# Wider rows for V, an earlier turn of one K tile, and two weight loads in another place

## The chip, the cores and the metric

The kernel runs on one core of one Trainium2 chip. The metric is device microseconds of one execution. All runs quoted here are of the fast state, with a granted TensorE clock of 0.997 to 1.0. A profile's span is 1.8 to 1.9 us shorter than the time of the same execution (188.6 us and 190.53 us for the profile of before). Engine names in the profile: PE is TensorE (matmul), PEld its weight loads, DVE VectorE, ACT ScalarE, POOL GpSimd, SP the engine that issues most loads.

## The reference

It is grouped-query attention over the last 2048 positions of a cache, with the projections before and after it.

```python
B, Sq, D = 8, 32, 1024;  Hq, Hkv, Sk, Dh = 32, 4, 8192, 128;  W = 2048
q = (x @ wq)                      # 8 query heads share one K/V head
scores = einsum(q, k_cache[:, :, Sk - W:]) * Dh ** -0.5
p = softmax(scores)
o = einsum(p, v_cache[:, :, Sk - W:])
out = o @ wo
```

There are 32 pairs of batch and K/V head, called units here. A unit has 256 query rows, 2048 keys and 512 KB each of K and V in bf16.

## The kernel before

The kernel takes a unit in four chunks ("slots") of 512 keys. In each slot TensorE computes four score matmuls, ScalarE takes the exponential, and two slots later TensorE multiplies by V in eight matmuls. V gets a column of ones, so the same matmuls also give the sum of the softmax: a row of V has 129 elements, 258 bytes.

```python
self.VW = self.Dh + 1                                    # 129
self.va = [self.c1.tile([P, self.KT, self.VW], BF16, name=f"va{i}") for i in range(3)]
...
for jj in range(CJ):                                     # the four rows of V of a chunk
    j = c * CJ + jj
    for qt in range(QT_N):                               # two matmuls with the same row of V
        nc.tensor.matmul(o_ps[:, qt, 0:self.VW], lhsT=pT[:, jj, qt * P:(qt + 1) * P], rhs=va[:, j, :], ...)
```

The score matmuls read K transposed. For most units the DMA transposes it. For units 0 to 4 TensorE does, and for units 5, 8, 11, ... the tile is turned beside TensorE: VectorE transposes blocks in four pieces (`kb`), then 16 moves put the blocks in place (`kTv`). For unit 5 GpSimd does twelve of the moves and VectorE four. A table names the slots:

```python
# unit: (load of K with that of unit .., blocks from, moves from, moves until, moves by GpSimd)
V_T = {5: (2, 6, 12, 17, 12), ...}
spread(blocks, s0, s1 + (s1 - s0) // 3)                  # unit 5: slots 6, 8, 10, 12
spread(moves, s1, s2)                                    # unit 5: slots 12 to 16
```

Projections for the next group of heads and output projections are cut into pieces and put between the slots. Their weights come by the same load queue as K and V; the n-th 512 KB of weights is issued after the loads of unit `W_AT[n]`:

```python
W_AT = (2, 3, 4, 4, 8, 8, 9, 10, 11, 12, ...)            # first four: group 1; next four: group 2
```

## Time and profile before

| | before |
|---|---|
| time, median of 3 runs | 189.4 us |
| span of the profiled execution | 188.6 us |
| PE busy | 181.3 us (96%) |
| ACT, DVE, POOL busy | 70%, 61%, 50% |
| idle gaps of PE, ended by DMA, POOL, DMA | 0.34, 0.71, 0.69 us |

From the page of before, its first two parts; a digit is the busy share of one fortieth of the span, in tenths:

```profile
PE 181.3 (96%) x2048; PEld 154.5 (82%) x2064; DVE 115.2 (61%) x267; ACT 131.9 (70%) x133; POOL 94.2 (50%) x150
PE   7999999989999899999999999999999999999993
```

PE is never far from full. Apart from the first and the last slice, its line has two weak ones, at 38 us and at 63 us. From the view of waits of before (who waited for whom; total us, times, longest us), the lines of PE, without that of the warm-up at the start (1.2 us):

```profile
PE s_ps L462 <- POOL kTv L255: 0.7, 1, 0.7
PE q_ps L269 <- DMA wq_sb<-in_wq_dram: 0.7, 1, 0.7
PE tp L230 <- DMA k_raw<-in_k_cache_dram: 0.3, 1, 0.3
```

Three stretches of the timeline of before show each of them (start, length, engine, line, operation, tiles; in brackets the idle time before it and what ended it):

```profile
24.66 0.34 PE L230 MATMUL tp<-ident,k_raw 128*128 128x128 bf16 x3 [0.34 <-DMA k_raw<-in_k_cache_dram]
...
30.54 8.37 POOL L255 TENSOR_SCALAR kTv<-kb 32x512 bf16<-32x512 bf16 x12 [28.97 <-PE o_ps L473]
...
38.96 0.28 PE L462 MATMUL s_ps<-QT_63,kTv 128*128 128x256 bf16 x1 [0.71 <-POOL kTv L255]
...
63.75 0.39 PE L269 MATMUL q_ps<-xT,wq_sb 128*128 128x256 bf16 x2 [0.69 <-DMA wq_sb<-in_wq_dram]
```

A gap in this view is shorter than what it costs, because a matmul's end is modelled and lies past the start of the next one (a matmul on V is 220 ns long in the profile, and the next one starts 56 to 61 ns after it). From start to start, less the usual distance, the three cost 0.50, 0.87 and 0.85 us.

The matmuls on V look alike in every view (median 220 ns each), but with the next start 56 to 61 ns on, that length is not what one costs. So the distance between starts says more. From the trace's records of before, mean ns from the start of a V matmul to the start of the next (the last one of a chunk is followed by other work, so that the figure of the second in row 3 comes from the one place where two chunks follow each other):

```text
row of the chunk           0      1      2      3
first matmul of the row   56.7   60.8   60.1   59.6
second                    56.6   55.9   55.9   56.0
```

### The profile page before, as it was taken

To read this page: it belongs to the slowest core of one execution; us is meant where nothing else is said; L and a number is where in the kernel's file an instruction comes from. 1 tells how busy PE (TensorE), PEld (TensorE's weight loads), DVE (VectorE), ACT (ScalarE), POOL (GpSimd) and SP (SyncE) were. 2 spreads that over 40 slices of the span, in tenths; PEclk is the share of its full clock that TensorE was granted. 3 is DMA by queue.
4 is the path that set the end of the run, shared out by engine and by line. 5 is a ranking of instruction groups with operands and counts; after the bars stand their busy time and mean duration, and the time that the engine had idled before them with its cause. 6 is when DMAs were issued, how large, how long until landed. Compare 5 with 4: busy or idle time off the path is not lost. (4 is left out here: it accounts for less than half of the span.)

```text
span 188.6 us, 5054 instructions
## 1 busy us (share of the span) xinstructions
PE 181.3 (96%) x2048; PEld 154.5 (82%) x2064; DVE 115.2 (61%) x267; ACT 131.9 (70%) x133; POOL 94.2 (50%) x150
## 2 busy tenths in 40 slices
PE   7999999989999899999999999999999999999993
PEld 2889989979999799987878899987787888888842
DVE  0137889994595485487367648756755865355272
ACT  2218889767789687878787686787777888888700
POOL 2000004959929939947963990697199279600000
DMA  4999999999999999999899999989999899960012
GB/s 161 301 384 412 402 402 386 201 233 335 301 198 280 378 264 293 358 262 290 284 377 207 363 380 292 275 289 386 257 368 333 231 260 287 272 149 0 3 59 63
DMA packets 52507, 51.75 MB, mean 274 GB/s; under 512 B 39424, under 2 KB 40064, under 8 KB 52480
## 3 DMA queue, kind: packets, MB, share of 16 engines
q1 hardware_dynamic: 51904, 50.87, 96.3%
q10 hardware_dynamic: 576, 0.52, 0.8%
q8 instruction: 17, 0.28, 0.6%
q14 instruction: 10, 0.08, 0.1%
HBM read 41.42 MB, written 0.52 MB: 222 GB/s over the span
## 5 line engine op out<-in xcount | busy, mean ns | idle before, releaser
L464 ACT ACTIVATE pT<-s_ps 128x1024 bf16<-128x1024 f32 x128 | 129.0, 1025 | 36.5 <-PE s_ps L462 35.5
L255 POOL TENSOR_SCALAR kTv<-kb 32x512 bf16<-32x512 bf16 x140 | 93.3, 666 | 68.7 <-PE o_ps L473 29.0
L473 PEld LDWEIGHTS <-pT 128*128 128x128 bf16 x1024 | 69.3, 98 | 3.1
L462 PEld LDWEIGHTS <-kT 128*128 128x128 bf16 x368 | 34.8, 98 | 10.3
L289 PE MATMUL op_ps<-wo_sb,OT 128*128 128x512 bf16 (+1 forms) x120 | 32.9, 365 | 0.8
L269 PE MATMUL q_ps<-xT,wq_sb 128*128 128x256 bf16 x192 | 28.3, 273 | 0.7 <-DMA wq_sb<-in_wq_dram 0.7
L473 PE MATMUL o_ps<-va_112,pT 128*128 128x129 bf16 x352 | 27.5, 220 | 0.0
L473 PE MATMUL o_ps<-va_113,pT 128*128 128x129 bf16 x352 | 27.3, 220 | 0.1
L473 PE MATMUL o_ps<-va_114,pT 128*128 128x129 bf16 x320 | 25.0, 220 | 0.0
L245 DVE STREAM_TRANSPOSE kb<-k_raw 128x512 bf16<-128x512 bf16 x36 | 23.9, 685 | 0.0
L411 DVE RECIPROCAL RL_all<-o_ps 128x2 f32<-128x2 f32 x32 | 5.3, 166 | 29.5 <-PE o_ps L473 29.2
L416 DVE TENSOR_SCALAR o_sb<-o_ps,RL_all 128x128 bf16<-128x128 f32 x64 | 19.5, 347 | 1.1
L462 PEld LDWEIGHTS <-kTv 128*128 128x128 bf16 x144 | 13.8, 98 | 6.1 <-POOL kTv L255 1.0
L269 PEld LDWEIGHTS <-wq_sb 128*128 128x128 bf16 x192 | 16.9, 98 | 2.1 <-DMA wq_sb<-in_wq_dram 1.0
L462 PE MATMUL s_ps<-QT_63,kT 128*128 128x256 bf16 x112 | 16.8, 273 | 0.0
L418 DVE STREAM_TRANSPOSE OT<-o_sb 128x256 bf16<-128x256 bf16 x32 | 14.3, 445 | 1.1
L462 PE MATMUL s_ps<-QT_66,kT 128*128 128x256 bf16 x96 | 14.4, 273 | 0.1
L289 PEld LDWEIGHTS <-OT 128*128 128x128 bf16 x136 | 11.1, 97 | 2.8 <-DVEq L76 0.6
L462 PE MATMUL s_ps<-QT_65,kT 128*128 128x256 bf16 x80 | 12.0, 273 | 0.1
L462 PE MATMUL s_ps<-QT_64,kT 128*128 128x256 bf16 x80 | 12.0, 272 | 0.1
L296 DVE TENSOR_TENSOR oacc<-op_ps,oacc 128x512 f32<-128x512 f32 x8 | 5.5, 682 | 7.5 <-PE op_ps L289 7.5
L405 DVE COPY va_113<-v_sb 128x2048 bf16<-128x2048 bf16 x11 | 9.0, 820 | 0.0
(46 smaller groups left out, 105.6 us busy)
## 6 DMA issues: line engine op xcount, KB each, us to landing
v_sb<-in_v_cache_dram SPq DMA_DIRECT2D x32, 512.0 KB, 7.3
wo_sb<-in_wo_dram SPq DMA_DIRECT2D x16, 512.0 KB, 6.7
wq_sb<-in_wq_dram SPq DMA_DIRECT2D x14, 512.0 KB, 7.5
k_raw<-in_k_cache_dram SPq DMA_DIRECT2D x13, 512.0 KB, 7.2
wq_sb<-in_wq_dram SPq DMA_DIRECT2D x4, 256.0 KB, 6.6
kT<-in_k_cache_dram SPq DMA_TRANSPOSE x36, 7.1
k_raw<-in_k_cache_dram SPq DMA_DIRECT2D x2, 256.0 KB, 7.9
x_sb<-in_x_dram ACTq DMA_DIRECT2D x1, 256.0 KB, 3.8
```

The costliest lines, as they stand in the source:

```text
L245: nc.vector.transpose(out=st["kb"][:, sl, :], in_=self.k_raw[ui][:, sl, :])
L255: nc.gpsimd.tensor_scalar(out=out, in0=in_, scalar1=1.0, scalar2=1.0, op0=ALU.mult, op1=ALU.mult)
L269: nc.tensor.matmul(st["ps"][:, 0:self.NQ], lhsT=self.wq_t[g, i][:, c % (DC // 2), hl * P:(hl + 1) * P], rhs=self.xT[:, c, :], start=(c == ...
L289: nc.tensor.matmul(ps[:, 0:w], lhsT=self.OT[:, gq, c, t * P:(t + 1) * P], rhs=self.wo_t[gq][:, c, n0:n0 + w], start=(k == 0), stop=(k == 7))
L296: nc.vector.tensor_tensor(out=acc, in0=ps[:, 0:w], in1=acc, op=ALU.add)
L405: self.nc.vector.tensor_copy(out=self.va[ui % 3][:, :, 0:self.Dh], in_=self.v_sb[ui][:, :, :])
L411: nc.vector.reciprocal(out=rl[:, ui * QT_N:(ui + 1) * QT_N], in_=o_ps[:, :, Dh])
L416: nc.vector.tensor_scalar(out=o_sb[:, qt, :, :], in0=o_ps[:, qt, 0:Dh].rearrange("p (i c) -> p c i", c=4), scalar1=rl[:, ui * QT_N + qt:ui ...
L418: nc.vector.transpose(out=self.OT[:, g * QT_N:(g + 1) * QT_N, :, b * self.Sq:(b + 1) * self.Sq], in_=o_sb[:, :, :, :])
L462: nc.tensor.matmul(s_ps[:, jj, :], lhsT=self.kT[ui][:, c * CJ + jj, :], rhs=q_u, start=True, stop=True)
L464: nc.scalar.activation(out=pT[:, :, :], in_=s_ps[:, :, :], func=ACT.Exp, bias=0.0, scale=self.scale)
L473: nc.tensor.matmul(o_ps[:, qt, 0:self.VW], lhsT=pT[:, jj, qt * P:(qt + 1) * P], rhs=va[:, j, :], start=(j == 0 and qt == 0), stop=(j == KT ...
```

## The change

It has four parts: a row of V becomes 160 elements (320 bytes), so that every row starts on a multiple of 64 bytes of its tile; the four block transposes of unit 5 move from slots 6, 8, 10, 12 to 5, 6, 8, 10, and its moves begin in slot 10 instead of 12; the first weights of group 1 are loaded behind K and V of unit 3 instead of unit 2; the last weights of group 2 behind the loads of unit 9 instead of 10.

```diff
+VA_ROW = 160
-V_T = {5: (2, 6, 12, 17, 12), ...
+V_T = {5: (2, (5, 6, 8, 10), 10, 17, 12), ...          # the other units keep their slots
-W_AT = (2, 3, 4, 4, 8, 8, 9, 10, 11, ...
+W_AT = (3, 3, 4, 4, 8, 8, 9, 9, 11, ...
-        self.va = [self.c1.tile([P, self.KT, self.VW], BF16, name=f"va{i}") for i in range(3)]
+        self.va = [self.c1.tile([P, self.KT, VA_ROW], BF16, name=f"va{i}") for i in range(3)]
...
-            spread(blocks, s0, s1 + (s1 - s0) // 3)
+            for k, p in enumerate(blocks):
+                plan[s0[k]].append(p)
...
-    ... rhs=va[:, j, :],
+    ... rhs=va[:, j, 0:self.VW],
```

More of the change, by code (lines that the diff above doesn't have):

```diff
@@ L20 @@
 N_WARM = (7, 0, 0)
+VA_ROW = 160
 PE_T = (0, 1, 2, 3, 4)
-V_T = {5: (2, 6, 12, 17, 12),
-       **{u: (u - 4, 4 * u - 16, 4 * u - 13, 4 * u - 4, 16) for u in (8, 11, 14, 17, 20, 23, 26, 29)}}
-W_AT = (2, 3, 4, 4, 8, 8, 9, 10, 11, 12, 13, 13, 14, 15, 16, 16, 18, 19, 19, 20, 22, 22, 23, 24, 25, 26, 28, 28)
+V_T = {5: (2, (5, 6, 8, 10), 10, 17, 12),
+       **{u: (u - 4, range(4 * u - 16, 4 * u - 12), 4 * u - 13, 4 * u - 4, 16) for u in (8, 11, 14, 17, 20, 23, 26, 29)}}
+W_AT = (3, 3, 4, 4, 8, 8, 9, 9, 11, 12, 13, 13, 14, 15, 16, 16, 18, 19, 19, 20, 22, 22, 23, 24, 25, 26, 28, 28)
 Q_SLOTS = {1: (17, 31), 2: (38, 54), 3: (69, 83)}
@@ L472, in pv @@
                         for qt in range(QT_N):
-                            nc.tensor.matmul(o_ps[:, qt, 0:self.VW], lhsT=pT[:, jj, qt * P:(qt + 1) * P], rhs=va[:, j, :],
+                            nc.tensor.matmul(o_ps[:, qt, 0:self.VW], lhsT=pT[:, jj, qt * P:(qt + 1) * P], rhs=va[:, j, 0:self.VW],
                                              start=(j == 0 and qt == 0), stop=(j == KT - 1), skip_group_check=True)
```

## The prediction

> **What bounds the kernel.** TensorE. The page has PE busy 181.3 of 188.6 us (96%), and the view of waits has three idle gaps of PE after the start-up: 0.34 us for the DMA of K of unit 3 (tp from k_raw, at 24.66 us), 0.71 us for GpSimd's last move of K of unit 5 (kTv, at 38.96), 0.69 us for the last weights of group 2 (wq_sb, at 63.75). Matmul ends overlap; by start-to-start intervals from the records those three cost 0.50, 0.87 and 0.85 us, 2.2 us together.
>
> **What the change does.**
>
> 1. *Weights of group 1 behind K and V of unit 3.* Early 512 KB loads land every 1.3 us (weights at 23.34, K of unit 3 at 24.62). K of unit 3 now lands near 23.4; PE needs it near 24.1. The 0.50 us goes. K of unit 4, next, still lands at 28.51, wanted near 28.55: no spare.
>
> 2. *Turn of unit 5 sooner.* GpSimd's 12 moves run from 30.54 to 38.91 (0.70 us each), behind VectorE's fourth transpose at 29.67. With that one in slot 10 it ends near 28.1, the moves near 36.5, and unit 5 is wanted near 37.5. The 0.87 us goes.
>
> 3. *Weights of group 2 one load sooner.* Issued at 57.77, they landed at 63.70; issued near 51, they land near 58.5. The 0.85 us goes. K of unit 14 lands 1.3 us later.
>
> 4. *Rows of 320 bytes.* The matmul on 129 columns of V runs 1024 times. From start to start it takes 56.6 ns for rows 0, 4, 8, 12 of V, whose byte offset (258 times the row) is a multiple of 8, but the first of each pair on the other rows takes 60.9, 60.1 and 59.5 ns (the second about 56). Per chunk of four rows that is 8.6 ns, in 128 chunks 1.1 us, all on PE. I take it for misalignment, which rows of 320 bytes remove. [...] The rival: the pattern follows the place within the chunk, also of period four; then nothing is gained. VectorE's copies of V (655 to 1090 ns) stay off the critical path.
>
> **What may be given back.** DMA engines are near 100% busy from 5 to 165 us (slices); loads hardly move with PE. The smallest spare time of V before its copy is 1.8 us (unit 16, landing 93.07, copy 94.87). PE will be about 2.8 us ahead there, so VectorE will wait about 1 us for V of units 15 to 17 and for K of units 14 and 20; PE itself has over 2 us more, so I count only 0.1 to 0.2 us.
>
> **Sum.** 189.4 - 2.2 - 1.0 + 0.2 = 186.4 us. Eight in ten: 185.7 to 187.6; near 187.3 if point 4 fails. Chances: faster by over 2% 0.12, within 2% 0.87, slower 0.01.
>
> **What would show it.** PE has no gap over 0.1 us near 24, 38 and 63; unit 5's first scores start near 37.4 instead of 38.96; groups of eight V matmuls start evenly at about 56.5 ns; the median of the copies of V stays near 690 ns.
>
> **What would make it wrong.** The row pattern is not alignment; VectorE, fully busy from 34 to 40 us, delays the earlier turn; K of unit 4 or V of unit 16 becomes the new wait, so that stalls move instead of going.

## The result, and the profile after

The changed kernel took 187.25 us (median of 6 runs, 187.13 to 187.44) against 189.41 us for the kernel before in the same rounds (6 runs, 188.68 to 189.69). The ratio is 0.989, with a 95% interval of 0.9871 to 0.9908. Here and below a ratio is the mean time of one kernel's fast runs over that of the other's fast runs of the same rounds, so it is not quite the ratio of the medians. The gain is 2.2 us. I had predicted 3.0 us: the time lies in the stated range (185.7 to 187.6), 0.85 us above its centre.

The page of after, the same two lines:

```profile
PE 178.8 (96%) x2048; PEld 153.1 (82%) x2064; DVE 115.1 (62%) x267; ACT 131.7 (71%) x133; POOL 94.7 (51%) x150
PE   7699999999999999999999999999999999999993
```

The weak slices at 38 and 63 us are gone; one in the start (4.6 to 9.3 us) is new. All lines of PE in the view of waits of after:

```profile
PE q_ps L372 <- DMA wq_sb<-in_wq_dram: 1.4, 1, 1.4
PE warm_ps L342 <- DVE wz L311: 1.2, 1, 1.2
```

The three waits of before are no longer there. The 1.4 us are in the first projection, at 6.8 us, where nothing was changed. The timeline of after at the places of the two large waits (start, length, as above):

```profile
28.59 8.78 POOL L256 TENSOR_SCALAR kTv<-kb 32x512 bf16<-32x512 bf16 x12 [27.02 <-DMA k_raw<-in_k_cache_dram]
...
37.65 0.60 PE L464 MATMUL s_ps<-QT_63,kTv 128*128 128x256 bf16 x4
...
61.25 0.60 PE L270 MATMUL q_ps<-xT,wq_sb 128*128 128x256 bf16 x4
```

GpSimd's moves begin 1.95 us sooner and end at 37.37 us; PE takes up unit 5 at 37.65 without a wait. It is a close fit: 0.29 us to spare, where I had expected 1.0. VectorE's fourth block transpose, for which the moves wait, before and after:

```profile
29.67 0.70 DVE L245 STREAM_TRANSPOSE kb<-k_raw 128x512 bf16<-128x512 bf16 x1
```

```profile
27.74 0.69 DVE L246 STREAM_TRANSPOSE kb<-k_raw 128x512 bf16<-128x512 bf16 x1
```

And the starts of the V matmuls, from the records of after:

```text
row of the chunk           0      1      2      3
first matmul of the row   56.6   56.5   56.7   56.6
second                    56.7   56.8   56.7   56.0
```

So in the profiles all four parts did what they were meant to do, and the spans differ by 3.0 us (188.6 and 185.6), exactly the gain I had predicted. That match is chance: after began its first score matmul 0.23 us later than before (13.65 and 13.43 us), and from there on the two differ by 3.27 us. The timed runs differ by 2.2 us only. That is the question for the experiments: 0.8 us that is in the pair of profiles and not in the pair of times. The profile of before belongs to an execution of 190.53 us, 1.1 us above the median of its timed runs.

Theory 1: the profile of before shows an unusual execution, in which loads were late; its two waits for a DMA (0.50 and 0.85 us) are not there in most runs. Theory 2: the waits are always there, and a part of the gain is lost elsewhere.

### The profile page after: what moved, and what is told of

Read it like the earlier page. It is cut to its first block, busy times and chain, and to the rows that moved or that the text cites. A ratio compares the mean times of both kernels' runs of the same rounds, so it can differ in the third digit from the quotient of the medians.

```text
span 185.6 us, 5054 instructions
## 1 busy us (share of the span) xinstructions
PE 178.8 (96%) x2048; PEld 153.1 (82%) x2064; DVE 115.1 (62%) x267; ACT 131.7 (71%) x133; POOL 94.7 (51%) x150
## 5 line engine op out<-in xcount | busy, mean ns | idle before, releaser
L475 PEld LDWEIGHTS <-pT 128*128 128x128 bf16 x1024 | 68.5, 98 | 3.1
L475 PE MATMUL o_ps<-va_112,pT 128*128 128x129 bf16 x352 | 27.1, 220 | 0.0
L475 PE MATMUL o_ps<-va_113,pT 128*128 128x129 bf16 x352 | 27.0, 220 | 0.1
L475 PE MATMUL o_ps<-va_114,pT 128*128 128x129 bf16 x320 | 24.7, 220 | 0.0
L406 DVE COPY va_113<-v_sb 128x2048 bf16<-128x2048 bf16 x11 | 9.5, 859 | 0.0
```

The costliest lines, as they stand in the source:

```text
L406: self.nc.vector.tensor_copy(out=self.va[ui % 3][:, :, 0:self.Dh], in_=self.v_sb[ui][:, :, :])
```

## The experiments

All twelve runs gave correct results. Each is the kernel before with the one edit shown, unless said otherwise. They ran in four jobs on four chips (4, 10, 12 and 14), each compared with before on the same chip. A gain in us is worked out from the ratio, unless said otherwise. "Cost" of a wait below is always from start to start.

### Which of the waits are there in every run

**before_again: the kernel before, profiled once more.** No edit.

> The kernel before, unchanged, profiled once more. Question: the change was worth 2.2 us in timed runs, 3.0 us between the two profiles, and I had predicted 3.0. Theory 1 (the profile of before that I costed from was of a slow run, 190.5 us against a median of 189.4, with loads landing every 1.29 us instead of 1.25): a profile of a usual run shows the same start intervals of V matmuls (56.6 and about 60 ns), the POOL gap of about 0.7 us near 38 again, but the two gaps that a DMA ends (0.34 near 24.7 and 0.69 near 63.7) smaller, all three together 1.0 to 1.4 us instead of 2.2. Theory 2 (the stalls are the same in every run, and part of the gain is lost elsewhere): the three gaps are again 2.2 us by start intervals. Time: 1.00 of before under both.

Measured: 189.66 us against 189.40, ratio 1.0011 (0.9995 to 1.0027). The view of waits of this second profile, the lines of PE but those of the start:

```profile
PE s_ps L462 <- POOL kTv L255: 0.7, 1, 0.7
```

The timeline of the second profile at the three places, K of unit 3, the turn of unit 5 and the weights of group 2:

```profile
24.44 0.39 PE L230 MATMUL tp<-ident,k_raw 128*128 128x128 bf16 x4
...
38.73 0.61 PE L462 MATMUL s_ps<-QT,kTv 128*128 128x256 bf16 x4 [0.71 <-POOL kTv L255]
...
62.45 0.60 PE L269 MATMUL q_ps<-xT,wq_sb 128*128 128x256 bf16 x4
```

The wait for GpSimd is there again, with the same cost (0.88 us). Both waits for a DMA are gone without any change of the kernel. The last weights of group 2 landed at 61.32 us instead of 63.70, before PE wanted them. The three together cost 0.88 us instead of 2.2, even less than theory 1 had said. From the first scores to the end of the span the two profiles of the same kernel took 175.21 us (188.64 - 13.43) and 173.84 us (187.54 - 13.70): a difference of 1.37 us, where the two missing waits are 1.35. The later jobs recorded the span of 44 executions of the kernel before, 186.8 to 188.1 us: the profile I had costed from, at 188.6, lies outside all of them.

**turn5_only: the earlier turn alone.**

```diff
-V_T = {5: (2, 6, 12, 17, 12), ...
+V_T = {5: (2, (5, 6, 8, 10), 10, 17, 12), ...           # with the placing of blocks by slot
```

> Before with only the turn of unit 5 two slots sooner. Theory 1 (of the three stalls only the one that GpSimd ends is there in every run): nearly all of the gain of the order, 0.8 to 1.0 us, ratio 0.9945 to 0.996; the gap near 38 gone. Theory 2 (the weights carry half of it): 0.4 to 0.6 us, ratio about 0.9975.

Measured: 188.55 us against 189.35, ratio 0.9964 (0.9948 to 0.998), a gain of about 0.7 us. That is between the two expectations. The wait for GpSimd is gone. But in this profile PE met the weights instead:

```profile
62.07 0.39 PE L270 MATMUL q_ps<-xT,wq_sb 128*128 128x256 bf16 x2 [0.45 <-DMA wq_sb<-in_wq_dram]
```

Those weights landed at 62.02 us and this wait cost 0.61 us; K of unit 3, landing at 24.06, cost 0.17. This profile is also one in which the first scores began early (13.20 us). It is one execution: whether the timed runs had these waits too, it does not tell.

**weights_only: the two weight moves alone.**

```diff
-W_AT = (2, 3, 4, 4, 8, 8, 9, 10, 11, ...
+W_AT = (3, 3, 4, 4, 8, 8, 9, 9, 11, ...
```

> Before with only the two weight moves. Theory 1: 0 to 0.3 us, ratio 0.998 to 1.000, because in a usual run the waits for K of unit 3 and for the last weights of group 2 are not there; the gap of 0.7 us that GpSimd ends near 38 stays. Theory 2: 0.5 to 1.3 us, ratio 0.993 to 0.997.

Measured: 188.99 us against 189.35, ratio 0.9984 (0.9968 to 0.9999). The gain is about 0.3 us and hardly clear of noise: theory 1. The profile keeps the wait for GpSimd (a gap of 0.70 us, at 38.32), and has none for a load after the start:

```profile
PE s_ps L464 <- POOL kTv L256: 0.7, 1, 0.7
```

**order_only: the turn and the weight moves, rows of 258 bytes.** Edit: after with `VA_ROW = 129`.

> The change without the rows: turn of unit 5 sooner and both weight moves, rows of 258 bytes. Theory 1: 1.0 to 1.3 us gained, ratio 0.993 to 0.995 (188.3 us), no gap of PE near 24, 38 and 63. Theory 2: 2.0 us gained, ratio 0.989, and then the two parts do not add up.

Measured: 188.22 us against 189.40, ratio 0.9948 (0.9928 to 0.9969), about 1.0 us (1.2 by the medians). PE has no gap over 0.1 us between 14 and 180 us. Turn (0.7) and weights (0.3) add up to it. Theory 2, which needed 2.0 us, falls.

**rows_turn: the whole change without the two weight moves**, and **after_again: the whole change, on the same chip.** Edit of the first, against after:

```diff
-W_AT = (3, 3, 4, 4, 8, 8, 9, 9, 11, ...
+W_AT = (2, 3, 4, 4, 8, 8, 9, 10, 11, ...
```

> The changed kernel without the two weight moves. In the profile of the earlier turn alone PE reached the last weights of group 2 about 0.9 us sooner than in a usual run of before and waited 0.45 us for them. If GpSimd's stall had hidden that wait, the wait is larger here, where PE comes another 0.5 us sooner: a gap of 0.5 to 1.2 us near 61 to 62, perhaps 0.2 us near 24, and 187.7 to 188.2 us, 0.4 to 0.9 us more than the whole change. If the weight moves are only worth what they are worth alone (0.2 to 0.3 us): 187.5 us.

> The changed kernel, unchanged, on the chip of the next two. Ratio 0.988 to 0.990 (187.3 us), no gap of PE over 0.1 us between 14 and 180 us in the profile, whatever the loads' pace.

Measured: after_again 187.02 us (186.76 to 187.71), ratio 0.9881; rows_turn 187.31 us (186.85 to 188.03), ratio 0.9889; before 189.42. My guess that the waits for weights would grow in this place is a miss: the difference is 0.1 to 0.3 us, inside the intervals (0.9859 to 0.9903 and 0.9865 to 0.9912). The profile of rows_turn shows no wait near 61 us at all; the weights landed at 61.54 and were wanted at 61.87. But that execution had lost time at the start, where PE waited for the first weights, and its first scores began at 14.06 us.

The view of waits of rows_turn, its first line of PE:

```profile
PE q_ps L372 <- DMA wq_sb<-in_wq_dram: 1.7, 2, 1.4
```

Put side by side, the profiles of kernels that do not have the weight moves show when the two waits come:

```text
                first     cost of the wait (us)       last weights of
                scores    K of unit 3   weights       group 2 landed
                (us)                    of group 2    (us)
pad_only        12.98     0.02          0.47          62.42
shift8_only     13.01     none          none          61.01
turn5_only      13.20     0.17          0.61          62.02
shift2_only     13.38     none          none          61.69
before          13.43     0.50          0.85          63.70
rows264_only    13.54     0.20          none          62.24
rows320_only    13.63     none          none          61.99
before_again    13.70     none          none          61.32
rows272_only    13.87     none          none          61.67
rows_turn       14.06     none          none          61.54
```

In four of ten executions at least one of the waits cost over 0.1 us. They come with a quick start or with late loads, but not with every quick start. The mean of the ten is 0.28 us, which is what the weight moves were worth alone (0.3 us). Why the start differs by 1.1 us and the landing by 2.7 us between executions, the runs do not tell; it is not only the chip, since 13.01 and 14.06 us were both on chip 12.

### What the rows of V do

**rows320_only: the rows alone.**

```diff
+VA_ROW = 160        # and rhs=va[:, j, 0:self.VW]
```

> Before with rows of 320 bytes alone. Theory 1: the 1.1 us of the V matmuls are gained nearly whole, ratio 0.994 to 0.996 (188.4 us), unless the waits for K of unit 3 and for weights grow because PE arrives sooner (up to 0.3 us given back). Theory 2 (gain lost elsewhere): ratio above 0.997.

Measured: 188.25 us against 189.40, ratio 0.994 (0.9923 to 0.9957), 1.15 us by the medians. All V matmuls start 56.6 to 56.7 ns apart. The groups of instructions show it too, in the busy time of the 1024 matmuls. First the second profile of before, then rows320_only (busy us, mean ns, idle before):

```profile
L473 PE MATMUL o_ps<-va,pT 128*128 128x129 bf16 x1024 | 79.8, 220 | 0.1
```

```profile
L475 PE MATMUL o_ps<-va,pT 128*128 128x129 bf16 x1024 | 78.8, 220 | 0.1
```

One microsecond less at an unchanged mean length. What PE gains before 38 us, though, the wait for GpSimd takes back: it cost 0.95 us here instead of 0.88. By the starts, the eight V matmuls of a chunk took 462.2 ns before and 454.4 now; 7.8 ns times 128 chunks are 1.0 us.

**rows264_only, rows272_only: two other widths.**

```diff
+VA_ROW = 132        # rows264_only
+VA_ROW = 136        # rows272_only
```

> Before with rows of 264 bytes alone: every row of V starts at a multiple of 8 bytes, half of them not of 16. If the cost is of starts off an 8-byte boundary, all matmuls on V start 56 to 57 ns apart and the time equals that of rows of 320 bytes within 0.1 us. If a 16-byte line counts, the odd rows stay near 58 to 61 ns and the gain is about half.

> Before with rows of 272 bytes alone, so that all rows start on a multiple of 16 and half of them not of 32. With rows of 264 bytes the rows at 8 past a multiple of 16 were still slow (60.8 ns). If the grain is 16 bytes: all matmuls on V start 56 to 57 ns apart, time as with 320 bytes (188.25 us, ratio 0.994). If it is 32 or 64: rows 1 and 3 of a chunk stay near 60 ns, ratio about 0.9965.

Measured: with 264 bytes 188.69 us, ratio 0.9964 (0.9946 to 0.9981); with 272 bytes 188.28 us, ratio 0.9946 (0.9928 to 0.9964). My reading in the prediction, that starts off a multiple of 8 bytes are what costs, falls here: with 264 bytes every start is a multiple of 8, and rows 1 and 3 of a chunk are as slow as before (60.8 ns), while row 2 is not (55.9). With 272 bytes nothing is slow. By the starts, 264 bytes save 2.7 ns a chunk, 0.35 us in all; by the time they saved 0.7 us, with an interval of 0.4 to 1.0 us, so that 0.35 lies at its lower edge.

**shift2_only, shift8_only: rows of 320 bytes, V put 2 or 8 bytes into each row.**

```diff
+VA_ROW = 160
+VA_AT = 1           # shift8_only: 4
-    rhs=va[:, j, :]
+    rhs=va[:, j, VA_AT:VA_AT + self.VW]       # the copy of V and the ones go there too
```

> Before with rows of 320 bytes, but V put 2 bytes into each row: the step is a multiple of 64, every start is off. If the start counts: the first matmul of rows 1, 2 and 3 of each chunk takes 60.9 ns each, 4.2 ns times 3 per chunk, 1.6 us more than rows of 320 bytes, so 0.5 us slower than before (ratio 1.002 to 1.003); and row 0 of a chunk tells whether it is free for its place (then 56.6) or was free for its start (then 60.9 too, 2.2 us more). If the step between rows counts and not the start: all 56 to 57 ns, ratio 0.994.

> Before with rows of 320 bytes and V put 8 bytes into each. With 2 bytes every matmul but the first of a chunk took 57.5 ns, not 56.6 and not 60.9. If any start off 16 costs that much: 57.5 ns again and ratio 0.999. If a start at 8 is free as long as all rows start alike: 56.6 ns and ratio 0.994. If a start at 8 is what cost 4 ns with rows of 264 bytes: 60.8 ns in rows 1 to 3, ratio 1.000 to 1.002.

Measured: shift2_only 188.96 us, ratio 0.9988 (0.997 to 1.0006); shift8_only 187.90 us, ratio 0.9922 (0.99 to 0.9945). Neither of the two answers I had written for 2 bytes came: its matmuls took 57.5 ns, all of them but the first of a chunk. With 8 bytes they took 56.6, as if nothing were off. The busy time of the 1024 matmuls, in the order of rows264_only, rows272_only, shift2_only and shift8_only:

```profile
L475 PE MATMUL o_ps<-va,pT 128*128 128x129 bf16 x1024 | 79.3, 220 | 0.1
...
L475 PE MATMUL o_ps<-va,pT 128*128 128x129 bf16 x1024 | 78.8, 220 | 0.1
...
L476 PE MATMUL o_ps<-va,pT 128*128 128x129 bf16 x1024 | 79.7, 222 | 0.1
...
L476 PE MATMUL o_ps<-va,pT 128*128 128x129 bf16 x1024 | 78.8, 220 | 0.1
```

The whole picture, from the records (mean ns from start to start of the first matmul of rows 0 to 3 of a chunk, and of all eight together, without the 11 or 12 of 128 chunks that a long matmul follows; starts of rows are counted from the start of the tile, whose own place in SBUF I did not read out):

```text
                 start of a row     row 0   row 1   row 2   row 3   eight
                 within 16 bytes
258 (before)     0, 2, 4, ... 14    56.7    60.8    60.1    59.6    462.2
264              0 and 8            56.7    60.8    55.9    60.8    459.5
320 + 2          always 2           56.7    57.5    57.5    57.5    459.9
320 + 8          always 8           56.7    56.6    56.7    56.7    454.5
272              always 0           56.7    56.6    56.7    56.7    454.5
320              always 0           56.7    56.7    56.6    56.7    454.4
```

What follows: the place within the chunk alone (the rival in the prediction) is out, since the same places are fast in the last three kernels. The step between rows alone is out (320 + 2 and 320 differ, and with 264 bytes row 2 is fast at the same step as its slow neighbours). The start of a row alone is out as well: a row at 8 is slow with 264 bytes and free with 320 + 8. In these six layouts a row costs 3 to 4 ns where it starts off a multiple of 16 and at another place within 16 bytes than the row before it; the first row of a chunk, which follows a score matmul or other work, never does (56.7 ns in all six). That is a description, and it leaves out the 0.9 ns that each matmul but the first of a chunk costs at 320 + 2. Why it should be so, no run shows; starts other than these were not tried with equal rows. Rows that all start on a multiple of 16 bytes (320, 272) were free of it (56.6 to 56.7 ns).

### Do the loads come sooner because of the rows?

The profiles held a second effect that I had not looked for. Two loads of 512 KB in a row (from K of unit 2 to K of unit 5) landed 1.28 us apart in all six profiles with rows of 258 or 264 bytes, and 1.23 us apart in all seven with 272 or 320. Chips 4 and 10 each show both. A load that comes sooner could itself be a gain.

**pad_only: rows of 258 bytes in tiles as large as those of 320.**

```diff
-        self.va = [self.c1.tile([P, self.KT, self.VW], BF16, name=f"va{i}") for i in range(3)]
+        va = [self.c1.tile([P, self.KT * 160], BF16, name=f"va{i}") for i in range(3)]
+        self.va = [v[:, 0:self.KT * self.VW].rearrange("p (k w) -> p k w", w=self.VW) for v in va]
```

> Before with each of the three V tiles as large as with rows of 320 bytes, but the rows themselves still 258 bytes apart (the rest of the tile is unused). In the profiles so far two 512 KB loads in a row (K of unit 2 to K of unit 5) landed 1.28 us apart in all six kernels with rows of 258 or 264 bytes, and 1.23 us apart in all seven with 272 or 320. If that comes from where the tiles that are loaded lie in SBUF after the larger V tiles: 1.23 us here too. If it comes from the rows that TensorE reads and VectorE writes: 1.28 us. Either way the V matmuls stay slow (60.9, 60.1, 59.5 ns in rows 1 to 3 of a chunk), the gap of 0.7 us near 38 stays, and the time stays within 0.3 us of before (ratio 0.998 to 1.001): then the gain of the rows is TensorE's and not the loads'.

Measured: 189.12 us against 189.33, ratio 0.999 (0.9971 to 1.0009). The V matmuls are slow as before (60.8, 60.2, 59.5 ns), and the loads land 1.23 us apart. Its V matmuls in the view of groups:

```profile
L474 PE MATMUL o_ps<-va,pT 128*128 128x129 bf16 x1024 | 79.8, 220 | 0.1
```

The view by windows of the stretch from 20 to 25 us, where the DMA share is over 1: first the second profile of before, then pad_only (at the end of a line: clock, DMA share, GB/s):

```profile
20.00:25.00 5.00, 5.00 (x74) 4.78 (x72) 4.20 (x10) 4.55 (x5) 0.00 (x0) 1.00 1.05 402
```

```profile
20.00:25.00 5.00, 5.00 (x76) 4.78 (x74) 4.31 (x9) 4.43 (x5) 0.00 (x0) 1.00 1.04 415
```

So the quicker loads do not need the rows that TensorE reads; they come with the larger tiles. Why, no run shows: the addresses in SBUF I did not read out, and this is one profile, on a chip (14) where before was not profiled. In all 14 profiles a V tile has 4128 or 4224 bytes per partition where the loads land 1.28 us apart, and 4352 or 5120 bytes where they land 1.23 us apart; no run tests what about the tiles counts. The time is hardly touched (ratio 0.999). The gain of the rows is TensorE's: 1.0 us by the starts of the V matmuls (rows320_only), which pad_only leaves slow (59.5 to 60.8 ns in rows 1 to 3).

## Why the prediction was right or wrong

**The sum.** From the first scores to the end of the span, the second profile of before took 173.84 us and after 171.95 (185.60 - 13.65). The difference, 1.90 us by the unrounded figures, is the wait for GpSimd (0.88) and the V matmuls (462.2 - 454.5 = 7.7 ns, times 128: 0.99) and 0.03 us of rest. With about 0.3 us from the weight moves this is the measured 2.2 us. The parts measured alone, 1.15 (rows), 0.7 (turn) and 0.3 (weights), also add up to it, but each has an interval of about 0.3 us on either side, so that the close match says little. Against these the prediction counted 1.05 us too much for the weights and took off 0.2 us that were not lost; the difference is the 0.85 us by which it missed.

**Points 1 and 3, the weights: the terms that were mis-sized.** "The 0.50 us goes" and "The 0.85 us goes" were true of the profile, but not of the usual run. Together I counted 1.35 us; alone they measured 0.3 us, with an interval that nearly reaches zero. The step that failed was before the mechanism: I costed from a single execution, of 190.53 us, although the timed runs of the same kernel stood beside it at 189.28 to 189.42. That difference of 1.1 us should have been in the estimate. A wait for a load is the first candidate for it, since landings move from one execution to the next: K of unit 3 landed at 24.62 and at 24.36 us in the two profiles of before, the last weights of group 2 at 63.70 and 61.32.

**Point 2, the turn: right.** Predicted 0.87 us; the profiles of before show 0.87 and 0.88, and after none. Alone, the turn measured 0.7 us, with an interval of 0.4 to 1.0 us. It may be that PE then sometimes meets the loads, as in its profile; that any of the 0.87 us is lost is not shown. Only the spare time was off: 0.29 us instead of 1.0, since VectorE's fourth transpose ended at 28.43 (27.74 + 0.69), not near 28.1, and the twelve moves took 8.78 us, not 8.37 (8.77 and 8.38 in the second profiles). Why the moves took longer was not looked into.

**Point 4, the rows: right in size and in that the starts of the rows count, wrong in which.** Predicted 1.0 to 1.1 us; 0.99 by the starts, 1.15 by the time of the rows alone. The rival is out. But "a multiple of 8" is not the condition, as the rows of 264 bytes show (60.8 ns in rows 1 and 3), nor is the start within 16 bytes alone, as those shifted by 8 show (56.6 ns).

**What may be given back: nothing was.** I had V of unit 16 late for its copy by about 1 us. It landed at 88.66 us in the profile of after, 3.73 us ahead of the copy. In after_again it was 2.00 us, and the smallest spare time after the start was 0.98 us (unit 17). The spare time of 1.8 us was that of the slow execution: in the second profile of before V of unit 16 landed at 89.46 us, 4.33 us ahead of its copy. "Loads hardly move with PE" was my estimate, from the DMA engines near 100% busy in the slices, and stays open: V of the last unit landed at 167.63 and 165.25 us in the two profiles of before, and at 163.52 and 165.38 in the two of after, so one kernel's executions differ as much as the kernels. The 0.2 us that I took off were too cautious, but small.

**What would show it.** No gap of PE at the three places: so in both profiles of after. Unit 5 from 37.4 us: 37.65 and 37.38. V matmuls even at about 56.5 ns: 56.6. The median of the copies of V near 690 ns: 683 and 684 (689 before).

## What to carry to other kernels

Compare the time of the profiled execution with the timed runs before costing its waits: here what it was slower by lay in waits for loads that most other runs do not have, while the wait for GpSimd came back in all nine profiles without the earlier turn (0.87 to 0.96 us). Look at the distance from start to start of repeated matmuls, by place in the loop; an instruction's length hid 4 ns here that cost 1 us in 1024 matmuls. Rows of a whole number of 16 bytes (272 and 320) took 454.5 and 454.4 ns for the eight matmuls of a chunk here, against 462.2 with 258 bytes; where a matmul reads rows of an odd width such as 129 columns, they are cheap to try.
